# Hedgehog attention with a gated MLP on one core: the third token tile taken from the transposed copy of x, tiles 4 and 5 split one tile sooner, and the key-value products in five runs

## The chip, the core and the metric

The kernel runs on one core of one Trainium2 chip. The metric is the device time of one execution in microseconds (us), lower is better. Runs of this kernel differ by a few tenths of a microsecond.

## What is computed

x holds 2048 tokens of 640 numbers. It is normalised token by token (`xn = layernorm(x)`), and two branches use the result:

```python
q, k, v = split(xn @ wqkv)                 # 32 heads of 20 numbers
phi_q = [softmax(q @ w_phi), softmax(-q @ w_phi)]      # 40 numbers a head; phi_k likewise
kv = phi_k^T v ;  z = sum of phi_k         # sums over all 2048 tokens
s  = (phi_q kv / (phi_q z + 1e-6)) @ wo
g  = silu(gelu(xn @ w1 + b1) @ w2 + b2)
out = x + s * g
```

All is float32. The products are made of rounded parts: each operand is split into a high part (rounded) and a low part (what the rounding left), and a product takes the three passes high-high, high-low and low-high.

## The kernel before, in words

**Tiles and stages.** The tokens stand in 16 tiles of 128 (t = 0 to 15), two tiles make a pair (q = t // 2). The first stage, some 237 us long, makes for every tile the key features (`project(t, wk_s)`, `feat1`, `feat2`, `key_fin`), the values (`value(t)`, later `value_pair`), the query features, and the sums kv. Then come twelve units of the MLP (TensorE lines L987 and L1016) and the closing products with wo. This case touches the first stage alone.

**How a tile of x becomes an operand.** TensorE needs the normalised x with its 640 features on the partitions, split in high and low. There are two ways to it:

- *By transposing* (tiles 0, 1 and 2 before the change): the tile `xt` is loaded token by token, VectorE (DVE) makes mean and variance (`norm_a`, lines L220 to L222; the power -1/2 is GpSimd's, POOL, L223), ScalarE (ACT) or VectorE normalises it, TensorE transposes it with five products with the identity (`transpose_x`, L383), and `plain` copies the high part out (ACT, L272) and subtracts for the low part (DVE, L274).
- *From the transposed copy of x* (tile 3 alone, then by pairs): `one_load` loads the columns of the tile, `xr`, from the transposed copy of x in DRAM. Mean and factor stand one token to a partition, but are needed along the free dimension, the same on every partition. So `one_stats` writes them to DRAM (`st_dram`, L361), and reads them back into all 128 partitions (`bc`, L363); between the two SyncE's queue (SP) waits until the writing has landed. Then POOL subtracts the mean (`one_sub`, L370), DVE multiplies (`one_plain`, L374), and `plain` splits. A pair of tiles goes the same way: `load_xr` (L252, L253), `pair_stats` (L220 to L225, store L322, read-back L324), `pair_sub` (POOL, L331, two instructions), `pair_mul` (DVE, L336), `pair_plain`.

**What a tile's products need.** `project` and `value` take a tile's split x as the stationary operand: 30 products of 128x320 each (L397). Their result stands in one of three PSUM buffers (`bankA`), and the buffer is needed again three uses later: a key tile's is free when `feat1` has read it (DVE: maximum, difference, minimum, L409 to L415), a value tile's when ACT has copied it out (L454). `feat1` ends with a subtraction on POOL (L416), `feat2` is the exponential on ACT (L425), `key_fin` the sums and the reciprocal on DVE (L433, L465) and the scaling on POOL (L438).

**The products for kv.** `kv_acc` (L477) adds a tile's part of phi_k^T v: 64 small products of 32x40, each on 32 of TensorE's 128 columns. `kv_pair` makes two tiles in a row, 128 products, and stands at eight places of the order, one for each pair.

**Order.** The start, through tile 5 and further, is written out by hand for all engines: each engine takes its instructions in the order of the program, and one that waits holds back all that is behind it. SP issues nearly all loads and stores of this stage, in one queue, also in that order. `folds` (L156) are the weights of which `fold_pair` (TensorE L164, DVE L187 and L188) makes the query weights; their PSUM buffers are of the same three.

Of the kernel before, what the change touches and what calls it, by code (L numbers as in the profile page):

```python
# [16 lines left out]
NT = S // P  # L17
# [29 lines left out]
def hedgehog_gated_mlp_kernel(ctx: ExitStack, tc: tile.TileContext, x, xt_in, wqk, bd, wv, wo, w1, b1, w2, b2, out_t):  # L47
    nc = tc.nc
# [181 lines left out]
    def norm_a(t):  # L230
        sm = small.tile([P, 16], F32, tag="st", name="st")
        nrm[t] = sm, stats(t, sm, None, sm[:, 14:15])
# [136 lines left out]
        bc, xr = pld[t, "one"], xrs[t, "one"]  # L369
        nc.gpsimd.tensor_tensor(xr, xr, bc[:, None, :, 0].to_broadcast([P, KC, P]), op=OP.subtract)  # L370

    def one_plain(t):
        bc, xr = pld.pop((t, "one")), xrs.pop((t, "one"))
        nc.vector.tensor_tensor(xr, xr, bc[:, None, :, 1].to_broadcast([P, KC, P]), op=OP.mult)  # L374
        plain(t // 2, t % 2, xr)

    def transpose_x(t):
        q, o = divmod(t, 2)
# [101 lines left out]

    vs, es, phis, xns, wk_s, wq_s = {}, {}, {}, {}, [], [None] * 4

    def kv_pair(t):
        for u in (t, t + 1):
            kv_acc(u, phis.pop(u), vs.pop(u))

    def load_w1(g):
# [45 lines left out]
    def x_in(t, eng=None):  # L533
        xts[t] = load_x(t, eng)
# [13 lines left out]
    wv_raw = [load_raw(wv[c * P:(c + 1) * P, :]) for c in range(KC)]  # L548
    for t in (3, 4, 5):
        x_in(t)  # L550
    x_in(6)
    x_in(7)
    nc.sync.dma_start(b1t[:], b1)
    nc.sync.dma_start(b2t[:], b2)
    wv_s = []

    def split_v(c):
# [11 lines left out]
    norm_a(1)  # L569
    fold_w(wkT, range(4, KC), "wk", wk_s)  # L570
    norm_act(1)
    norm_a(2)
    st3 = one_stats(3)
    next(st3)
    split_v(0)
    one_load(3)
    kvp[0] = bankB("kv")
    pk = project(0, wk_s, lambda: transpose_x(1), 4)
    split_v(1)
    next(st3)  # L580
    load_xr(2)
    norm_act(2)
    split_v(2)
    es[0] = feat1(pk)
    split_v(3)
    pk = project(1, wk_s, lambda: transpose_x(2))
    split_v(4)
    feat2(es[0])
    es[1] = feat1(pk)
    one_sub(3)  # L590
    pair_stats(4)
    vs[0] = value(0)
    pair_stats(5)
    wqT = load_fold(0, (nc.sync,) * KC)
    x_in(8)
    x_in(9)
# [3 lines left out]
    one_plain(3)  # L600
    phis[0] = key_fin(es.pop(0))
    vs[1] = value(1)
    phis[1] = key_fin(es.pop(1))
    vf = [v_forms(0), v_forms(1)]
    for t in range(2, 6):
        pk = project(t, wk_s)
        if t % 2:
            kv_pair(t - 3)
        es[t] = feat1(pk)
        if t == 4:  # L610
            next(vf[0])
        if t == 2:
            pair_sub(2)
            pair_stats(6)
            pair_stats(7)
            pair_mul(2)
        if t == 3:
            pair_plain(2)
        if t > 3:
            pair_stats(t + 4)  # L620
        if t in (3, 4, 5):
            spill(t - 3)
        if t == 5:
            x_in(10)
        if t == 4:
            pair_sub(3)
            pair_mul(3)
        vs[t] = value(t)
        if t >= 4:
            fold_pair(t - 4)  # L630
        if t == 5:
            next(vf[0])
        feat2(es[t])
        if t == 4:
            pair_plain(3)
        phis[t] = key_fin(es.pop(t))
# [122 lines left out]
    for t in range(6, 10):  # L759
        q = t - 3  # L760
        pk = project(t, wk_s)
        if t == 8:
            kv_pair(6)
            spill(3)
        if t == 9:
            vb = value_forms(sv_raw, [nc.vector, nc.vector, nc.gpsimd, nc.gpsimd])
            w_dump(0)
            w_dump(1)
        if t == 6:
            next(vf[1])  # L770
        es[t] = feat1(pk)
        if t > 6:
            feat2(es[t])
            if t < 9:
                pair_mul(q)
                pair_plain(q)
                t_sums(q)
        else:
            pair_sub(4)
            fold_w(wqT, range(4, KC), "wq", wq_s)  # L780
            feat2(es[t])
        if t < 8:
# [24 lines left out]
        if t == 9:  # L807
            for _ in range(4):
                next(vb)
        if t == 7:  # L810
            pair_sub(5)
        if t < 9:
            store_e(queries_done.pop(0), ef)
        if t == 6:
            kv_pair(4)
        for u in XIN.get(t, ()):
            x_in(u)
    qf, later, last_sums = None, [], []
# [18 lines left out]
    for p in range(5, 8):  # L837
        t = 2 * p
# [4 lines left out]
            next(qf)  # L843
        es[t] = feat1(pk)
        pk = project(t + 1, wk_s)
        if p > 6:
            kv_pair(t - 2)
        es[t + 1] = feat1(pk, later)
        if p == 5:
            value_pair(4, {1: first_store, 2: lambda: next(vb, None), 4: x_mid, 5: lambda: plain_hi(6), 6: x_low})  # L850
# [9 lines left out]
        def between(p=p):  # L860
            if p == 5:
                load_xr(7)
                pair_stats(14)
                pair_stats(15)
            if p < 7:
                kv_pair(2 * p - 2)

        def rest(t=t, p=p):
            later.pop(0)()
# [53 lines left out]
    for q in range(4, 8):  # L923
# [4 lines left out]
            hooks[4] = last_key  # L928
        ea, eb = token_pair(q, wq_b, wq_f, hooks, later)
        if q == 5:  # L930
            kv_pair(NT - 2)
            kvr = kv_rest()
    later.pop(0)()
    e_14, e_last = ea, eb
# [685 lines left out]
```

## Time and profile before

| what | value |
|---|---|
| median of the runs | 639.14 us (639.01 to 639.66) |
| the profiled execution | 637.78 us, its span 636.1 us |
| TensorE busy | 631.3 us, 99% of the span |
| VectorE, GpSimd, ScalarE busy | 511.1, 432.5 and 259.7 us |
| DMA, mean over the span | 215 GB/s |

In the profile PE is TensorE's products and PEld its weight loads; DVE is VectorE, ACT ScalarE, POOL GpSimd, SP SyncE, and a q behind a name is the engine's issuing queue. A row of the timeline has the start, the busy time, the engine, the line, the operation, what it writes and reads, and in brackets for how long the engine stood idle ahead of it and what ended that. The chain is the work that ended last, followed back from the end. All times are from the start of the span.

### The profile page before, as it was taken

How to read it: one execution, taken by the hardware profiler on the slowest of the kernel's cores; microseconds unless marked ns; L12 is line 12 of the kernel's file. 1: busy time of each engine (PE TensorE's matmuls, PEld its weight loads, DVE VectorE, ACT ScalarE, POOL GpSimd, SP SyncE). 2: the span in 40 equal slices, each digit the busy share in tenths (PEclk: the TensorE clock that was granted, in tenths of full speed). 3: DMA queues.
4: the chain of work that ended last, by engine and by line, in shares of the span. 5: the costliest groups of instructions: out<-in, count | busy, mean ns of one | idle time of the engine just before them, and what ended most of it. 6: DMA issues, size and time to landing. Idle time of an engine off the chain costs nothing.

```text
span 636.1 us, 11441 instructions
## 1 busy us (share of the span) xinstructions
PE 631.3 (99%) x4324; PEld 550.3 (87%) x4324; DVE 511.1 (80%) x790; ACT 259.7 (41%) x390; POOL 432.5 (68%) x376
## 2 busy tenths in 40 slices
PE   9999999999999999999999999999999999999997
PEld 9999999999999998888888888888888888667676
DVE  5887976789887877878979869758798899887586
ACT  3522422334344347243442534842322335455540
POOL 1877466888978857687878876381735678866363
PEclk9999999999999999999999999999999999999999
DMA  9577287393421488359899699697498598969934
GB/s 347 121 227 230 75 286 223 100 344 134 90 76 42 131 304 284 111 106 349 212 287 315 162 385 350 135 319 258 138 245 168 172 176 271 306 181 310 377 110 152
DMA packets 167168, 136.90 MB, mean 215 GB/s; under 512 B 89864, under 2 KB 130824, under 8 KB 166728
## 3 DMA queue, kind: packets, MB, share of 16 engines
q1 hardware_dynamic: 164376, 124.56, 65.9%
q10 hardware_dynamic: 2736, 11.60, 4.7%
q8 instruction: 34, 0.56, 0.4%
q14 instruction: 22, 0.18, 0.1%
HBM read 87.76 MB, written 48.38 MB: 214 GB/s over the span
## 4 chain that ended last, share of the span: by engine, by line
PE 98%; DMA 1%; DVE 0%; SPq 0%; issue 0%
PE pB L1016 26%; PE pB L987 23%; PE pA L397 22%; PE pB L1218 10%; PE pA L710 7%; PE pB L1144 3%; PE pA L164 2%; PE qV L710 2%; PE kv L477 2%; PE qY L710 1%; DMA folds<-in_wqk_dram 1%; PE pB L1126 0%; PE pA L383 0%; DVE y L1228 0%; PE pB L942 0%; DVE xres L1229 0%
## 5 line engine op out<-in xcount | busy, mean ns | idle before, releaser
L1016 PE MATMUL pB<-hs,w2s 128*128 128x512 f32 x720 | 165.9, 389 | 0.0
L1016 PEld LDWEIGHTS pB<-hs,w2s 128*128 128x128 f32 x720 | 135.0, 188 | 28.8 <-issue 0.8
L987 PE MATMUL pB<-xp,w1s 128*128 128x512 f32 x324 | 81.4, 389 | 0.0
L987 PE MATMUL pB<-xd,w1s 128*128 128x512 f32 x324 | 79.3, 389 | 0.0
L438 POOL TENSOR_TENSOR eq<-eq,rc 128x1280 f32<-128x1280 f32 x16 | 37.9, 2371 | 60.6 <-DVE rc L1078 48.4
L987 PEld LDWEIGHTS pB<-xp,w1s 128*128 128x128 f32 x324 | 60.7, 188 | 12.8 <-ACT x L1003 0.3
L987 PEld LDWEIGHTS pB<-xd,w1s 128*128 128x128 f32 x324 | 60.8, 188 | 12.6
L1025 DVE TENSOR_TENSOR y<-pB,y 128x512 f32<-128x512 f32 x100 | 63.1, 675 | 1.8 <-PE pB L1016 1.8
L992 ACT ACTIVATE pB<-pB,b1t 128x512 f32<-128x512 f32 x48 | 31.8, 662 | 77.3 <-DVE pB L1418 29.5
L397 PE MATMUL pA<-wk,xp 128*128 128x320 f32 x384 | 59.6, 310 | 0.0
L425 ACT ACTIVATE e<-e 128x1280 f32<-128x1280 f32 x32 | 40.7, 1271 | 43.3 <-POOL e L416 42.8
L397 PEld LDWEIGHTS pA<-wk,xp 128*128 128x128 f32 x384 | 56.9, 188 | 0.1
L416 POOL TENSOR_TENSOR e<-nr,e 128x640 f32<-128x640 f32 x32 | 44.8, 1402 | 15.9 <-DVE nr L415 15.5
L438 POOL TENSOR_TENSOR e<-e,rc 128x1280 f32<-128x1280 f32 x16 | 38.4, 2407 | 21.0 <-DVE rc L465 21.0
L1065 POOL TENSOR_TENSOR ez<-eq,zrep 128x1280 f32<-128x1280 f32 x16 | 47.4, 2962 | 2.8 <-DMA eq<-e_dram 2.8
L505 POOL TENSOR_TENSOR w1s<-raw,w1s 128x640 fp32r<-128x640 f32 (+1 forms) x18 | 25.4, 1410 | 18.0 <-ACT w1s L504 17.7
L139 POOL TENSOR_TENSOR w2s<-raw,w2s 128x640 fp32r<-128x640 f32 x23 | 36.1, 1589 | 0.2 <-ACT w2s L137 0.2
L998 DVE TENSOR_TENSOR hs<-pB,hs 128x512 fp32r<-128x512 f32 x48 | 32.0, 683 | 3.8 <-ACT hs L994 3.6
L137 ACT ACTIVATE w2s<-raw 128x640 fp32r<-128x640 f32 x24 | 17.2, 735 | 41.5 <-DVE dn L433 12.1
L409 DVE TENSOR_REDUCE mx<-pA 128x32 f32<-128x640 f32 x32 | 25.9, 809 | 8.9 <-PE pA L397 8.6
L994 ACT ACTIVATE hs<-pB 128x512 fp32r<-128x512 f32 x48 | 28.8, 600 | 2.1
L397 PE MATMUL pA<-wq,xp 128*128 128x320 f32 x192 | 29.6, 309 | 0.0
(220 smaller groups left out, 1281.0 us busy)
## 6 DMA issues: line engine op xcount, KB each, us to landing
raw<-in_w_dram SPq DMA_DIRECT2D x42, 320.0 KB
e_dram<-e ACTq DMA_DIRECT2D x16, 640.0 KB
eq<-e_dram SPq DMA_DIRECT2D x16, 640.0 KB
phi_t<-eq SPq DMA_DIRECT2D x64, 160.0 KB
phT<-phi_t SPq DMA_DIRECT2D x20, 512.0 KB
xt<-in_x_dram SPq DMA_DIRECT2D x16, 320.0 KB
xres<-in_xt_dram SPq DMA_DIRECT2D x20, 256.0 KB
out_dram<-xres SPq DMA_DIRECT2D x19, 256.0 KB
```

The source lines that it names most:

```text
L139: eng.tensor_tensor(sl[:, 1, :], raw, sl[:, 0, :].bitcast(F32), op=OP.subtract)
L397: nc.tensor.matmul(ps[:, hf, :HALF], stat_x(q, o, k, a), ws[k][:, b, hf * HALF:(hf + 1) * HALF], start=n == 0, stop=n == 3 * KC - 1)
L416: rest = lambda: nc.gpsimd.tensor_tensor(e5[:, :, :, 1, :], nr[:, :, :, None].to_broadcast([P, 2, 16, DH]), e5[:, :, :, 0, :], op=OP.subtract)
L425: nc.scalar.activation(ef, ef, AF.Exp)
L438: nc.gpsimd.tensor_tensor(e3, e3, rc[:, :, None].to_broadcast([P, 64, DH]), op=OP.mult)
L710: nc.tensor.matmul(bank[ch], q_x(blk, a, q), p_weight(base, f, w, k)[:, b], start=ch not in seen and n == 0, stop=n == len(mms) - 1, skip_ ...
L987: nc.tensor.matmul(bank[ch][:], tl[:, a, off + wo_:off + wo_ + P], mov(blk, b), start=new and n == 0, stop=n == len(mms) - 1, skip_group_c ...
L998: nc.vector.tensor_tensor(hs[:, 1], ps, hs[:, 0].bitcast(F32), op=OP.subtract)
L1016: nc.tensor.matmul(ps[:], ws[i][:, b, d * P:(d + 1) * P], hs[o][i][:, a, :], start=i == n == 0, stop=(i, n) == (GF - 1, 2), skip_group_che ...
L1025: nc.vector.tensor_tensor(y, ps[:], y, op=OP.add)
L1065: nc.gpsimd.tensor_tensor(zv, ef, zf, op=OP.mult)
L1218: nc.tensor.matmul(ps[:, mv], w, o[:, mv], start=first and n == 0, stop=last and n == len(steps) - 1, skip_group_check=True)
```

## The change

Three things are changed.

1. Tile 2 is no longer transposed on TensorE. It goes by `one_load(2)`, `one_stats(2)`, `one_sub(2)`, a multiplication on DVE (`one_mul`, cut out of `one_plain`) and `plain`, whose low part stands behind `pair_stats(5)` on DVE. The loads of b1 and b2 move from ahead of tile 3's statistics to behind their read-back, and tile 3's `one_load` from ahead of the statistics' stores to between those of tile 2 and of tile 3.
2. The subtraction and the split of the pair 2 (tiles 4 and 5) come sooner: `pair_sub(2)` ahead of `key_fin` of tile 1, `pair_plain(2)` in the loop's turn for tile 2, not 3.
3. The key-value products are made in five runs: tiles 0 to 3, 4 to 7, 8 and 9, 10 to 13, 14 and 15. `kv_pair(t)` becomes `kv_tiles(*ts)`.

```diff
     def one_mul(t):
         bc, xr = pld.pop((t, "one")), xrs.pop((t, "one"))
         nc.vector.tensor_tensor(xr, xr, bc[:, None, :, 1].to_broadcast([P, KC, P]), op=OP.mult)
-        plain(t // 2, t % 2, xr)
+        return xr
+
+    def one_plain(t):
+        plain(t // 2, t % 2, one_mul(t))
...
-    def kv_pair(t):
-        for u in (t, t + 1):
+    def kv_tiles(*ts):
+        for u in ts:
             kv_acc(u, phis.pop(u), vs.pop(u))
...
     for t in (3, 4, 5):
         x_in(t)
+    one_load(2)
     x_in(6)
     x_in(7)
-    nc.sync.dma_start(b1t[:], b1)
-    nc.sync.dma_start(b2t[:], b2)
...
     norm_act(1)
-    norm_a(2)
+    for _ in one_stats(2):
+        pass
     st3 = one_stats(3)
     next(st3)
+    one_load(3)
     split_v(0)
-    one_load(3)
     kvp[0] = bankB("kv")
     pk = project(0, wk_s, lambda: transpose_x(1), 4)
     split_v(1)
     next(st3)
+    nc.sync.dma_start(b1t[:], b1)
+    nc.sync.dma_start(b2t[:], b2)
     load_xr(2)
-    norm_act(2)
     split_v(2)
     es[0] = feat1(pk)
     split_v(3)
-    pk = project(1, wk_s, lambda: transpose_x(2))
+    pk = project(1, wk_s)
     split_v(4)
+    one_sub(2)
     feat2(es[0])
     es[1] = feat1(pk)
     one_sub(3)
     pair_stats(4)
+    x2 = one_mul(2)
     vs[0] = value(0)
+    plain(1, 0, x2, lo=False)
     pair_stats(5)
+    plain(1, 0, x2, hi=False)
...
     vs[1] = value(1)
+    pair_sub(2)
     phis[1] = key_fin(es.pop(1))
...
         pk = project(t, wk_s)
-        if t % 2:
-            kv_pair(t - 3)
+        if t == 5:
+            kv_tiles(0, 1, 2, 3)
...
         if t == 2:
-            pair_sub(2)
             pair_stats(6)
             pair_stats(7)
             pair_mul(2)
-        if t == 3:
             pair_plain(2)
...
         if t == 8:
-            kv_pair(6)
+            kv_tiles(4, 5, 6, 7)
             spill(3)
```

The other three places where a `kv_pair` stood are treated in the same way.

In SP's queue this is the part from the first loads of x to the read-back for the pair 2 before the change (`xt` is x by tokens, `xr` columns of the transposed copy, `st_dram` the store of the statistics, `bc` their read-back; L347 is `one_load(3)`, L361 and L363 are tile 3's store and read-back, L322 and L324 the pair's):

```order
L132 DMA xt<-in_x_dram 128x640 x5
L553 DMA b1t<-in_b_dram 128x12
L554 DMA b2t<-in_b_dram 128x5
L347 DMA xr<-in_xt_dram 128x5x128
L361 DMA st_dram<-st 128x2
L363 DMA bc<-st_dram 128x256
L252 DMA xr<-in_xt_dram 128x5x128
L253 DMA xr<-in_xt_dram 128x5x128
L322 DMA st_dram<-pst 128x2x2
L324 DMA bc<-st_dram 128x512
```

And this is the same part after it; the first L347 and the first L361 and L363 are tile 2's, the second ones tile 3's:

```order
L132 DMA xt<-in_x_dram 128x640 x3
L347 DMA xr<-in_xt_dram 128x5x128
L132 DMA xt<-in_x_dram 128x640 x2
L361 DMA st_dram<-st 128x2
L363 DMA bc<-st_dram 128x256
L347 DMA xr<-in_xt_dram 128x5x128
L361 DMA st_dram<-st 128x2
L363 DMA bc<-st_dram 128x256
L584 DMA b1t<-in_b_dram 128x12
L585 DMA b2t<-in_b_dram 128x5
L252 DMA xr<-in_xt_dram 128x5x128
L253 DMA xr<-in_xt_dram 128x5x128
```

A second store and read-back now stand ahead of tile 3's, and tile 3's load stands between the two.

On POOL this is the part from tile 3's subtraction to the first subtraction of `feat1` for tile 2, before the change (L223 is the power for tiles 4 and 5, L438 the scaling of `key_fin`, here for tiles 0 and 1, L331 the pair 2):

```order
L416 TENSOR_TENSOR e<-nr,e 128x32x20
L370 TENSOR_TENSOR xr<-xr,bc 128x5x128
L223 TENSOR_TENSOR pst<-pst,mhalf 128x1
L447 MEMSET v 128x32
L448 MEMSET v 128x32
L223 TENSOR_TENSOR pst<-pst,mhalf 128x1
L438 TENSOR_TENSOR e<-e,rc 128x1280
L447 MEMSET v 128x32
L448 MEMSET v 128x32
L438 TENSOR_TENSOR e<-e,rc 128x1280
L416 TENSOR_TENSOR e<-nr,e 128x32x20
L331 TENSOR_TENSOR xr<-xr,bc 128x5x128 x2
```

And after it, behind tile 2's subtraction (L370 is still tile 3; L419 and L441 are the lines that were L416 and L438):

```order
L419 TENSOR_TENSOR e<-nr,e 128x32x20
L370 TENSOR_TENSOR xr<-xr,bc 128x5x128
L223 TENSOR_TENSOR pst<-pst,mhalf 128x1
L450 MEMSET v 128x32
L451 MEMSET v 128x32
L223 TENSOR_TENSOR pst<-pst,mhalf 128x1
L441 TENSOR_TENSOR e<-e,rc 128x1280
L450 MEMSET v 128x32
L451 MEMSET v 128x32
L331 TENSOR_TENSOR xr<-xr,bc 128x5x128 x2
L441 TENSOR_TENSOR e<-e,rc 128x1280
L419 TENSOR_TENSOR e<-nr,e 128x32x20
```

The pair's subtraction now stands ahead of the scaling of tile 1 and of tile 2's subtraction in `feat1`, and those two are behind it.

More of the change, by code (lines that the diff above doesn't have):

```diff
@@ L370, in one_sub, with one_mul @@
         nc.gpsimd.tensor_tensor(xr, xr, bc[:, None, :, 0].to_broadcast([P, KC, P]), op=OP.subtract)
-    def one_plain(t):
+    def one_mul(t):
         bc, xr = pld.pop((t, "one")), xrs.pop((t, "one"))
         nc.vector.tensor_tensor(xr, xr, bc[:, None, :, 1].to_broadcast([P, KC, P]), op=OP.mult)
-        plain(t // 2, t % 2, xr)
+        return xr
+    def one_plain(t):
+        plain(t // 2, t % 2, one_mul(t))
     def transpose_x(t):
@@ L813, in hedgehog_gated_mlp_kernel @@
             store_e(queries_done.pop(0), ef)
-        if t == 6:
-            kv_pair(4)
         for u in XIN.get(t, ()):
@@ L845, in hedgehog_gated_mlp_kernel @@
         pk = project(t + 1, wk_s)
-        if p > 6:
-            kv_pair(t - 2)
+        if p == 7:
+            kv_tiles(10, 11, 12, 13)
         es[t + 1] = feat1(pk, later)
@@ L864, in between @@
                 pair_stats(15)
-            if p < 7:
-                kv_pair(2 * p - 2)
+            if p == 5:
+                kv_tiles(8, 9)
         def rest(t=t, p=p):
@@ L930, in hedgehog_gated_mlp_kernel @@
         if q == 5:
-            kv_pair(NT - 2)
+            kv_tiles(14, 15)
             kvr = kv_rest()
```

## The prediction

> **What bounds the kernel now.** I read the chain of work that ended last, then TensorE's own waits over the whole span.
>
> ```profile
> PE 98%; DMA 1%; DVE 0%; SPq 0%; issue 0%
> ```
> ```profile
> PE pA L541 <- PEq L1610: 0.8, 1, 0.8
> PE pA L164 <- DMA folds<-in_wqk_dram: 0.2, 1, 0.2
> ```
>
> TensorE is the chain, and past the first 8 us it waits for nothing. So whatever time TensorE's own work loses comes off the end, and every wait that the change gives it is added. The other engines have slack, but an unknown amount, so the question is whether the new path of tile 2 still delivers in time. The profiled execution took 637.78 us, 1.36 below the median of the three timed runs (639.14); I sum against it and carry the difference to the median.
>
> **What TensorE saves.** The chain in order of time has the transposes of tile 2, and a run of kv products with its neighbours:
>
> ```profile
> 20.65 0.55 PE pA L383 x5
> 21.20 23.76 PE pA L397 x162
> ...
> 62.32 4.40 PE pA L397 x30
> 66.72 1.32 PE kv L477 x124
> 68.04 4.59 PE pA L397 x30
> ```
>
> The transposes' 0.55 us go. The kv products stay, but three runs fewer are begun and ended. The 30 products behind a run take 4.59 us, against 4.40 elsewhere: a run costs 1.32 + 0.19 = 1.51. Inside a run, counted in two windows that start together:
>
> ```profile
> 45.10:45.30 0.20, 0.20 (x44) 0.20 (x33) 1.00 0.95 356
> 45.10:45.70 0.60, 0.60 (x89) 0.60 (x78) 1.00 1.02 370
> ```
>
> 45 more in 0.4 us is 8.9 ns each, 1.14 us for 128. So a run's two ends cost 1.51 - 1.14 = 0.37 us (at least the 0.19 that shows behind it), and three runs fewer give 1.1 (0.6 to 1.1). Together TensorE saves 1.65 us. If all else stays hidden, that is the result.
>
> **What the other engines lose: tile 2's trip through DRAM.** Here are SP's issues for tile 3 (20.77, 23.94), for the pair 2 (31.69, 34.94) and for the pair 3 (46.36, 51.64). Each read-back is issued when its store has landed. Below them, the bytes that moved in two windows.
>
> ```profile
> 20.77 0.34 SPq L361 DMA_DIRECT2D st_dram<-st  x1
> 23.94 0.33 SPq L363 DMA_DIRECT2D bc<-st_dram  x1
> 24.32 0.43 SPq L252 DMA_DIRECT2D xr<-in_xt_dram  x1
> ...
> 31.69 0.37 SPq L322 DMA_DIRECT2D st_dram<-pst  x1
> 34.94 0.34 SPq L324 DMA_DIRECT2D bc<-st_dram  x1
> ...
> 40.10 0.38 SPq L252 DMA_DIRECT2D xr<-in_xt_dram  x1
> ...
> 46.36 0.82 SPq L322 DMA_DIRECT2D st_dram<-pst  x1
> 51.64 0.34 SPq L324 DMA_DIRECT2D bc<-st_dram  x1
> ```
> ```profile
> 24.30:27.30 3.00, 3.00 (x22) 3.00 (x22) 2.90 (x6) 1.28 (x1) 2.41 (x2) 1.00 0.69 18
> 27.30:30.40 3.10, 3.10 (x23) 3.10 (x22) 1.50 (x8) 1.87 (x2) 1.98 (x3) 1.00 0.92 244
> ```
>
> A store's trip is 3.17 and 3.25 us, and 5.28 for the third, which was issued behind four loads of xr. And the loads issued at 24.3 moved next to nothing (18 GB/s) until 27.3, while the read-back ahead of them ran; then they ran at 244. So the queue serves in order of issue, loads and stores alike: what stands behind a read-back waits 3.4 us from that one's issue. POOL's rows give the read-backs' landing and what follows:
>
> ```profile
> 16.61 0.55 POOL L223 TENSOR_TENSOR st<-st,mhalf 128x1 f32<-128x1 f32 x1 [1.62 <-DVE st L222]
> ...
> 28.80 1.59 POOL L370 TENSOR_TENSOR xr<-xr,bc 128x640 f32<-128x640 f32 x1 [1.12 <-DMA bc<-st_dram]
> ...
> 37.28 2.37 POOL L438 TENSOR_TENSOR e<-e,rc 128x1280 f32<-128x1280 f32 x1
> 39.61 1.28 POOL L416 TENSOR_TENSOR e<-nr,e 128x640 f32<-128x640 f32 x1
> 40.84 3.15 POOL L331 TENSOR_TENSOR xr<-xr,bc 128x640 f32<-128x640 f32 x2
> ...
> 58.07 1.28 POOL L416 TENSOR_TENSOR e<-nr,e 128x640 f32<-128x640 f32 x1
> ```
>
> A read-back for a tile takes 28.80 - 23.94 = 4.86 us; for a pair 5.16 (34.94 until SP's next issue, which waited for it, at 40.10). Now the new order, step by step.
>
> - Tile 2's store can be issued at 17.2, when POOL's power is done. Two loads of 320 KB (its own xr and x_in(7)) are not yet through. Four cost the pair 3's store 2.1 us, so two cost 1.05: landed at 17.2 + 3.17 + 1.05 = 21.4 (20.4 with a free queue, 22.5 by the longest trip). Read-back 21.4 to 26.3; subtraction to 27.9. With 0.82 and 0.81 us on DVE and 0.74 on ACT (rows below, same shapes) it is split by about 30.3, or by 31.1 if DVE first finishes `pair_stats(5)`. TensorE needs it at 31.2: 72 of the 162 products (0.147 each) after 21.20, less 0.55. No wait, but no room.
> - Tile 3's store is issued 0.8 behind tile 2's read-back, at 22.2, and behind tile 3's xr. That load gets the queue at 21.4 + 3.4 = 24.8 and needs 320 KB at 244 GB/s, 1.3 us. The store follows at 26.1; of its trip the part after its turn is unknown, at most 3.2; I take 2.5: landed 28.6 (25.4 if nothing held it, 29.3 at most). Read-back to 33.5, where tile 3 had its own at 28.80.
> - The pair 2's powers stand behind tile 3's subtraction on POOL. SP's store came 2.89 us after that began (28.80 to 31.69), so now at 36.4; landed 39.6; read-back until 44.8. POOL subtracts until 47.95, where it ended at 43.99 before. That would be 4 us late, and what moved ahead makes it worse: tile 1's scaling (2.37) and tile 2's subtraction (1.28), which ran before 40.9, now come behind it.
>
> What follows is priced by these rows of DVE, ACT and PE:
>
> ```profile
> 44.02 1.49 DVE L336 TENSOR_TENSOR xr<-xr,bc 128x1280 f32<-128x1280 f32 x1 [2.43 <-POOL xr L331]
> ...
> 53.17 1.49 DVE L433 TENSOR_REDUCE rc<-e 128x64 f32<-128x1280 f32 x1 [0.59 <-ACT e L425]
> ...
> 56.14 0.82 DVE L412 TENSOR_TENSOR e<-pA,mx 128x640 f32<-128x640 f32 x1
> 57.00 0.82 DVE L415 TENSOR_REDUCE nr<-e 128x32 f32<-128x640 f32 x1
> ...
> 62.95 1.49 DVE L336 TENSOR_TENSOR xr<-xr,bc 128x1280 f32<-128x1280 f32 x1 [3.85 <-POOL xr L331]
> ...
> 66.86 0.49 DVE L188 TENSOR_TENSOR sr<-sr,pA 128x320 f32<-128x320 f32 x1
> ```
> ```profile
> 45.55 0.74 ACT L272 ACTIVATE xp<-xr 128x640 fp32r<-128x640 f32 x1 [3.09 <-DVE xr L336]
> ...
> 46.50 0.51 ACT L272 ACTIVATE xp<-xr 128x384 fp32r<-128x384 f32 x1
> ...
> 50.88 0.71 ACT L454 ACTIVATE v<-pA 128x640 f32<-128x640 f32 x1 [3.87 <-PE pA L397]
> 51.87 1.27 ACT L425 ACTIVATE e<-e 128x1280 f32<-128x1280 f32 x1 [0.28 <-POOL e L416]
> ```
> ```profile
> 50.68 4.56 PE L397 MATMUL pA<-wk,xp 128*128 128x320 f32 x30
> ...
> 67.97 2.02 PE L397 MATMUL pA<-wv,b 128*128 128x320 f32 x12
> ```
>
> - *Tile 4's projection.* `pair_mul(2)` ends at 49.45, the three high parts at 50.95 (45.51 to 47.01 before), and behind them, on ACT, stands the copy of tile 2's value, to 51.7. The projection takes that PSUM buffer. TensorE would be there at 50.68 - 0.55 - 1.51 (the kv run of tiles 0 and 1 is gone from here) = 48.6. First wait: 3.1 us.
> - *Tile 5's projection.* POOL comes to tile 2's subtraction at 50.3, ends at 51.6; exponential on ACT behind the copy, 53.0. DVE from the head sums to the end of the next tile's minimum: 53.17 to 57.82 before, 4.65, now 57.65. Tile 3's subtraction (1.28) and exponential: 60.2. From head sums to tile 4's difference, 3.79: 64.0. This frees the buffer that the projection takes; TensorE would be there at 62.32 - 2.06 + 3.1 = 63.4. Second wait: 0.6.
> - *Tile 5's value.* Tile 4's minimum ends at 64.85, then POOL's subtraction starts; pair 3's began 1.75 later (58.07, then 59.82) and DVE's multiplication 3.13 after that: 69.75. The query weights' differences that free the PSUM buffer end 4.40 after it (62.95 to 67.35): 74.15. TensorE would be there at 67.97 - 0.92 + 3.7 = 70.75. Third wait: 3.4.
>
> So value(5) starts at 74.15 instead of 67.97, 6.2 late; two more merged runs give back 0.74 later. Sum: +5.45, 643.2 against the profiled execution, **644.6** against the median.
>
> **Edits at nothing.** b1 and b2, first used after 230 us, and x_in(6), (7), used at 38.9: their later loads are covered. Phi and values held longer keep buffers: `load_xr(5)` now waits for tile 4's kv product.
>
> ```profile
> 117.68 1.39 PE L477 MATMUL kv<-e,v 128*32 128x40 f32 x128
> ```
>
> That is at 118.4 by this clock; a pair needs about 4 us, so POOL's `pair_sub(5)`, at 120.97 before, comes 1.5 late. That run is now 256 products and holds TensorE 1.14 us longer at the same place, so I price it at 0 (at most 1.5).
>
> **The rivals.**
>
> *A, the trips are covered.* The late chain costs nothing if the pair's read-back lands by 37.6 (44.8, less the 7.1 us that TensorE waits and 0.1); it breaks even at 39.3. Then the time is 639.14 - 1.65 = 637.5. For it: SP's store for tile 2 starts 3.5 us sooner than tile 3's did. Against: two trips in a row of 3.2 and 4.9, measured. The Trainium skill, "DMA: Bandwidth & Descriptors", section on the anatomy of one DMA, gives about 2.0 us and bytes at 436 GB/s for a DMA; that would be 2.3 us for tile 2's read-back and bring the pair's in time, 637.5. The rows (3.17 for 1 KB, 4.86 for 128 KB) do not agree, and they decide. Chance 0.17.
>
> *B, the store is not held.* Tile 3's store passes the read-back and the load ahead of it and lands at 25.4, 3.2 sooner. The first wait goes, value(5) starts at 70.95: +3.0 - 0.74, so 641.4. For it: I took the order of loads among themselves from a clear row, that of a store behind loads from one trip of 5.28. Chance 0.2, a quarter of it within 0.2% of 639.14.
>
> *C, the clock falls too.* The waits of 3.1 and 3.4 us are the first pauses of TensorE since the start; the granted clock is 1.00 in all windows above. If it fell to a half for as long as each wait lasted, half of 6.5 us more is lost: 647.9. No row here shows a lowered clock. The Trainium skill, "TensorE: Matmul & The Clock Gate", "Why this matters for your kernels", warns of just this for idle gaps above some 3 us; no run so far shows it. Chance 0.12.
>
> *The forecast* has what remains, 0.51.
>
> **How the numbers follow.** About 0.2%, 1.3 us, is what a measurement of this kernel can tell from no change. Faster is A, 0.16 of it beyond 1.3 us; within it a rest of A, B's quarter and a little of the forecast, 0.08; slower 0.76. The range leaves out A and B's lower end (some 0.19) and holds forecast, B and C: 640.0, since B with tile 2's store at 20.4 gives 641.4 - 1.0 and some of its buffers' slack, to 648.2, just above C; tile 2's store at 22.5 would add 1.1 to the forecast.
>
> **What would show it.** Right: DMA waits on POOL ahead of all three, tile 2's, tile 3's and the pair 2's subtraction, the last near 44.8; TensorE idle ahead of tile 4's projection (ended by ACT's copy of a value) and of tile 5's value (ended by DVE's L188 subtraction); kv runs without a pause of their own. Wrong: TensorE without a wait after 8 us, or the pair 2's read-back landing by 40, which would put the fault in the two trips; or a wait at tile 2's own projection at 31.2, which would put it in the first.

## The result, and the profile after the change

| | before | after |
|---|---|---|
| median of 6 runs, us | 639.12 (638.97 to 639.66) | 655.01 (651.26 to 657.85) |
| ratio | | 1.0247, 95% interval 1.0215 to 1.0278 |
| profiled execution, us (span) | 637.78 (636.1) | 656.25 (654.5) |
| mean granted clock of TensorE | 1.000 | 0.989 |

The change made the kernel 2.5% slower: 15.9 us by the medians, 18.4 by the two profiled spans. The forecast was 644.6, its range ended at 648.2. TensorE's waits (total, how often, longest):

```profile
PE pA L400 <- ACT v L457: 6.5, 1, 6.5
PE kv L480 <- issue: 6.2, 3, 2.4
PE pA L717 <- DVE v L731: 0.4, 1, 0.4
```

The first row is the wait at tile 4's projection, named in the forecast, twice as long. The second is new: TensorE stands idle three times *inside* the runs of key-value products, and what ends the idle time is "issue": nothing that the profile follows, no semaphore and no other engine. TensorE's timeline at these places (start, duration, line, products, idle time before):

```profile
55.59 6.54 PE L400 MATMUL pA<-wk,xp 128*128 128x320 f32 x30 [6.52 <-ACT v L457]
61.96 4.56 PE L400 MATMUL pA<-wv,xp 128*128 128x320 f32 x30
...
73.53 1.66 PE L480 MATMUL kv<-e,v 128*32 128x40 f32 x159
76.87 1.11 PE L480 MATMUL kv<-e,v 128*32 128x40 f32 x97 [1.68 <-issue]
...
126.12 2.07 PE L480 MATMUL kv<-e,v 128*32 128x40 f32 x202
130.59 0.70 PE L480 MATMUL kv<-e,v 128*32 128x40 f32 x54 [2.41 <-issue]
131.23 6.20 PE L400 MATMUL pA<-wq,xp 128*128 128x320 f32 x30
...
207.62 2.18 PE L480 MATMUL kv<-e,v 128*32 128x40 f32 x217
211.94 0.57 PE L480 MATMUL kv<-e,v 128*32 128x40 f32 x39 [2.14 <-issue]
```

Each of the three runs of 256 products breaks off once, after 159, 202 and 217 of them. The two runs of 128 have no break. And the 30 products behind the first wait take 6.54 us, those behind the second break 6.20, where 30 alike take 4.56. The windows say why. The column behind the five engines is the granted clock, as a share of the full one, on average over the window:

```profile
55.60:62.00 6.40, 6.40 (x31) 6.40 (x32) 4.84 (x7) 1.70 (x2) 4.08 (x6) 0.68 0.14 18
77.90:82.40 4.50, 4.50 (x38) 4.49 (x31) 4.47 (x7) 0.70 (x2) 0.41 (x1) 1.00 0.39 149
131.20:137.20 6.00, 6.00 (x40) 5.97 (x31) 3.83 (x5) 1.27 (x1) 5.37 (x4) 0.72 0.52 173
212.40:217.10 4.70, 4.70 (x32) 4.66 (x22) 0.00 (x0) 0.88 (x2) 1.28 (x2) 0.64 0.01 3
```

The clock is 0.68, 0.72 and 0.64 behind the first wait and the second and third break, and 1.00 behind the first break, the shortest (1.68). So each of these three pauses costs twice: its length, and 1.5 to 2 us of slower products.

How the first wait came to 6.5 us is in SP's issues (the store and read-back of tile 2, of tile 3, of the pair 2), in POOL's rows for tile 3 and the pair 2, and in DVE's multiplication and ACT's high part and value copy:

```profile
17.46 0.39 SPq L361 DMA_DIRECT2D st_dram<-st  x1
21.38 0.33 SPq L363 DMA_DIRECT2D bc<-st_dram  x1
...
22.30 0.46 SPq L361 DMA_DIRECT2D st_dram<-st  x1
28.91 0.32 SPq L363 DMA_DIRECT2D bc<-st_dram  x1
...
37.51 0.37 SPq L322 DMA_DIRECT2D st_dram<-pst  x1
42.02 0.34 SPq L324 DMA_DIRECT2D bc<-st_dram  x1
```
```profile
34.57 1.64 POOL L370 TENSOR_TENSOR xr<-xr,bc 128x640 f32<-128x640 f32 x1 [5.55 <-DMA bc<-st_dram]
...
46.63 3.17 POOL L331 TENSOR_TENSOR xr<-xr,bc 128x640 f32<-128x640 f32 x2 [3.47 <-DMA bc<-st_dram]
49.75 2.36 POOL L441 TENSOR_TENSOR e<-e,rc 128x1280 f32<-128x1280 f32 x1
```
```profile
49.83 3.63 DVE L336 TENSOR_TENSOR xr<-xr,bc 128x1280 f32<-128x1280 f32 x1 [2.42 <-POOL xr L331]
```
```profile
53.49 0.74 ACT L272 ACTIVATE xp<-xr 128x640 fp32r<-128x640 f32 x1 [14.96 <-DVE xr L336]
...
54.85 0.68 ACT L457 ACTIVATE v<-pA 128x640 f32<-128x640 f32 x1
```

The chain is the one of the forecast, link by link, and its links are longer towards the end: tile 2's trip as worked out, tile 3's read-back 1.1 late, the pair's store 4.51 us under way where 3.2 was taken, the subtraction done at 49.80 (47.95). The store's packets moved from 38.39 to 38.63, so 3.4 us lie between its last packet and its landing, where 2.1 did in the kernel before; the cause of that is open. Then DVE's multiplication of the pair, 1.49 us before, takes 3.63: POOL's scaling began 0.08 us ahead of it and ended at 52.11, and 52.11 + 1.49 = 53.60 is about where DVE ends (53.46).

Where the 18.4 us are, by the difference between the starts of the same product of TensorE in the two traces:

| place | us |
|---|---|
| wait at tile 4's projection | +6.6 |
| lower clock behind it | +2.0 |
| key-value runs: breaks 6.23, all runs together (breaks included) | +6.2 |
| lower clock behind the second and third break | +3.0 |
| tile 2's transposes | -0.5 |
| small waits (0.6 ahead of L717's products, and others) | +1.0 |

So the tile and the runs cost about half each, and over a quarter of the loss is the clock. This is the bill of one execution: the six had granted clocks of 0.989 to 0.996, and the one with 0.996 was the shortest (651.26).

### The profile page after: what moved, and what is told of

Its sections match the earlier page's. It is cut to its first block, busy times and chain, and to the rows that moved or that the text cites. A ratio compares the mean times of both kernels' runs of the same rounds, so it can differ in the third digit from the quotient of the medians.

```text
span 654.5 us, 11441 instructions
## 1 busy us (share of the span) xinstructions
PE 636.1 (97%) x4319; PEld 554.9 (85%) x4319; DVE 516.0 (79%) x791; ACT 258.7 (40%) x389; POOL 433.4 (66%) x377
## 4 chain that ended last, share of the span: by engine, by line
PE 86%; DMA 6%; DVE 3%; POOL 2%; issue 2%; ACT 0%; SPq 0%; DVEq 0%; POOLq 0%
PE pB L1021 25%; PE pB L992 22%; PE pA L400 15%; PE pB L1223 10%; PE pA L717 5%; PE pB L1149 3%; DMA bc<-st_dram 2%; PE pA L164 1%; PE kv L480 1%; PE qV L717 1%; DMA st_dram<-pst 1%; DVE xr L336 1%; DMA st_dram<-st 1%; DMA folds<-in_wqk_dram 1%; PE qY L717 1%
## 5 line engine op out<-in xcount | busy, mean ns | idle before, releaser
L441 POOL TENSOR_TENSOR eq<-eq,rc 128x1280 f32<-128x1280 f32 x16 | 37.9, 2371 | 60.6 <-DVE rc L1083 43.8
L400 PE MATMUL pA<-wk,xp 128*128 128x320 f32 x384 | 61.4, 316 | 6.5 <-ACT v L457 6.5
L400 PEld LDWEIGHTS pA<-wk,xp 128*128 128x128 f32 x384 | 58.7, 194 | 6.9 <-ACT v L457 6.8
L419 POOL TENSOR_TENSOR e<-nr,e 128x640 f32<-128x640 f32 x32 | 44.2, 1384 | 16.9 <-DVE nr L418 11.0
L441 POOL TENSOR_TENSOR e<-e,rc 128x1280 f32<-128x1280 f32 x16 | 37.8, 2367 | 21.0 <-DVE rc L468 21.0
L400 PE MATMUL pA<-wq,xp 128*128 128x320 f32 x192 | 31.1, 320 | 0.0
L400 PEld LDWEIGHTS pA<-wq,xp 128*128 128x128 f32 x192 | 30.0, 197 | 0.1
```

What stands on the lines that cost most here:

```text
L400: nc.tensor.matmul(ps[:, hf, :HALF], stat_x(q, o, k, a), ws[k][:, b, hf * HALF:(hf + 1) * HALF], start=n == 0, stop=n == 3 * KC - 1)
L419: rest = lambda: nc.gpsimd.tensor_tensor(e5[:, :, :, 1, :], nr[:, :, :, None].to_broadcast([P, 2, 16, DH]), e5[:, :, :, 0, :], op=OP.subtract)
L441: nc.gpsimd.tensor_tensor(e3, e3, rc[:, :, None].to_broadcast([P, 64, DH]), op=OP.mult)
```

## What breaks the runs: three experiments

**Theory.** The page's list of DMA queues has one that carries instructions in large pieces:

```profile
q8 instruction: 34, 0.56, 0.3%
```

34 packets, 0.56 MB: 16 KB each. TensorE's instructions in the trace, loads of weights, matmuls, semaphore instructions and drains, are 8,742, so 64 bytes and 256 to a packet. Counted from the first, the breaks stand behind instructions 1217, 2497 and 4289: five and seven times 256 apart, exactly. So TensorE's program seems to come in blocks of 256 instructions, and one block is used up before the next is there. The three packets that end the breaks start at 74.44, 128.01 and 209.72, each 1.0 to 1.1 us long, and TensorE goes on 1.3 to 1.4 us behind their end. A block of the usual products lasts 128 x 0.147 = 19 us; one of key-value products 1.4. **Rivals:** the break comes from a run's length, or has to do with tile 2's late data.

**Five runs alone.** The kernel before, with only this part of the change:

```diff
-        if t % 2:
-            kv_pair(t - 3)
+        if t == 5:
+            kv_tiles(0, 1, 2, 3)
...
-            kv_pair(6)
+            kv_tiles(4, 5, 6, 7)
...
-        if p > 6:
-            kv_pair(t - 2)
+        if p == 7:
+            kv_tiles(10, 11, 12, 13)
```

> The kernel before with only the key-value products in five runs; tile 2 is transposed on TensorE as before. Theory (TensorE's instructions come in blocks of 256, and a run of 256 products, 512 instructions at about 10 ns a product, uses one whole block up in 1.3 us, before the next is there): a pause of 1.7 to 2.4 us in each of the three merged runs, not at a fixed product, but where a block ends. Counted over the loads of weights, matmuls and semaphore instructions, that is at products 153, 196 and 210 of the 256 (give or take 2), where the changed kernel had 159, 202 and 217, because ten instructions of transposes stand ahead; with it a lower granted clock behind those over 2 us; together about 639.1 - 1.1 + 6.2 + 3.1 = 647.3 (645 to 649). No wait at tile 4's projection. Rival (the pauses in the changed kernel follow from tile 2's late data, or from the run's length alone): none here, 638.0; or at products 159, 202 and 217 again.

Measured: 647.42 (646.76 to 650.7) against 637.76 of the kernel before on that chip; ratio 1.0141 (1.0101 to 1.0181). The three merged runs in its timeline:

```profile
65.40 1.61 PE L477 MATMUL kv<-e,v 128*32 128x40 f32 x153
68.74 1.17 PE L477 MATMUL kv<-e,v 128*32 128x40 f32 x103 [1.73 <-issue]
...
118.05 2.02 PE L477 MATMUL kv<-e,v 128*32 128x40 f32 x196
122.90 0.77 PE L477 MATMUL kv<-e,v 128*32 128x40 f32 x60 [2.84 <-issue]
...
199.36 2.13 PE L477 MATMUL kv<-e,v 128*32 128x40 f32 x211
203.97 0.63 PE L477 MATMUL kv<-e,v 128*32 128x40 f32 x45 [2.48 <-issue]
```

The breaks come after 153, 196 and 211 products, as forecast (153, 196, 210), not after 159, 202 and 217; and they stand again behind instructions 1217, 2497 and 4289. Tile 2 is transposed here, so its late data have no part in it. The clock fell behind the break of 2.84 us (0.72 from 123.6 to 129.6), not behind the one of 2.48. The time grew by 9.7 us, where I gave 8.2: the breaks are 7.0 in all and the lower clock costs 1.5, half of what I had; and the 1.1 us that I took as saved by fewer runs are not there.

**Runs of three tiles.** If a block's end decides, runs of one length must differ.

```diff
-        if t % 2:
-            kv_pair(t - 3)
+        if t == 5:
+            kv_tiles(0, 1, 2)
...
-            kv_pair(4)
+            kv_tiles(3, 4, 5)
...
-        if p > 6:
-            kv_pair(t - 2)
+        if p == 7:
+            kv_tiles(10, 11, 12)
...
-            kv_pair(NT - 2)
+            kv_tiles(13, 14, 15)
```

> The kernel before with the products in six runs: of the tiles 0 to 2, 3 to 5, 6 and 7, 8 and 9, 10 to 12, 13 to 15, so four runs of 192 products alike. Theory (a run pauses where a second block of 256 instructions would begin inside it): counted from the kernel before, blocks end at product 25, 27, 82 and 110 of the four, and the next ones 128 products later: at 153 and 155 of the first two, behind the end of the other two. So a pause of 1.7 to 2.8 us in the first two, at those products, and none over 0.5 in the last two; the time is 2 to 7 us above the kernel before. Rival (a run of over 128 products pauses by its length): a pause in all four, or in none, and at like products.

Measured: 645.70 (643.41 to 646.45) against 638.82, ratio 1.0110 (1.0093 to 1.0127). The four runs of 192:

```profile
66.71 1.61 PE L477 MATMUL kv<-e,v 128*32 128x40 f32 x153
70.09 0.57 PE L477 MATMUL kv<-e,v 128*32 128x40 f32 x39 [1.77 <-issue]
...
96.79 1.63 PE L477 MATMUL kv<-e,v 128*32 128x40 f32 x155
100.42 0.56 PE L477 MATMUL kv<-e,v 128*32 128x40 f32 x37 [2.00 <-issue]
...
198.73 1.97 PE L477 MATMUL kv<-e,v 128*32 128x40 f32 x192
...
224.69 1.98 PE L477 MATMUL kv<-e,v 128*32 128x40 f32 x192
```

Four runs alike in length: breaks in the first two, at the products forecast, none in the other two. So a rule of length does not hold. The median is 6.9 us above the kernel before. The profiled execution (643.41, the fastest of four) shows 3.8 in the two breaks and a wait of 1.1 at tile 4's projection, to which TensorE comes 1.3 sooner, since the first run has been moved behind it. Its granted clock was 1.000; that of the other three, 1.6 to 3.0 us longer, was 0.994 to 0.997.

**As many instructions, each longer.** The changed kernel, each key-value product 320 columns wide; the sums kv are then other ones.

```diff
-                nc.tensor.matmul(ps[32 * e:32 * e + 32, 40 * s:40 * s + 40], v[:, 21 * h:21 * h + 32],
-                                 phi[:, 40 * h:40 * h + 40], ...
+                nc.tensor.matmul(ps[32 * e:32 * e + 32, :320], v[:, 21 * h:21 * h + 32],
+                                 phi[:, 320 * (s // 2):320 * (s // 2) + 320], ...
```

> The changed kernel with each key-value product 320 columns wide, not 40 (the key-value matrix then holds other sums, eight heads' products each): as many instructions in the same five runs, but each takes about 35 ns if four of them still run beside each other (a quarter of the 147 ns of a 128x320 product), not 10. Theory (the next block of instructions comes some 3 to 4 us after the one before it was begun): 256 instructions now last 4.5 us, so the three merged runs have no pause over 0.5 us; the time grows by the products, some 1024 x 0.025 = 26 us, less 6 to 9 of pauses and clock: about 672. Rival (a run of 256 products in this tile shape pauses whatever it lasts): three pauses of about 2 us again.

Measured: 705.01, one run. Its first merged run, in one piece:

```profile
73.30 17.43 PE L480 MATMUL kv<-e,v 128*32 128x320 f32 x256
```

No run breaks off, and TensorE's only long wait is the one at tile 4's projection (6.3). A product takes 68 ns, not 35, so the time is 33 us above what I gave. On the question asked, the theory holds: with as many instructions in a run, and each one longer, the break is gone. The Trainium skill, "Runtime: NRT & Kernel Launch", section "Instruction fetch mechanics", describes the blocks of 256 instructions, with the next one fetched while the present one runs, and calls the cost mostly hidden. The traces agree on the blocks; that they are hidden holds here for products of 147 and of 68 ns, not of 10.

## What the third tile costs: five experiments

**Tile 2 alone, eight runs.** The first run stands behind tile 4's projection, since tile 1's features come later now.

```diff
-        if t == 5:
-            kv_tiles(0, 1, 2, 3)
+        if t > 3:
+            kv_tiles(2 * t - 8, 2 * t - 7)
...
```

The other runs of four tiles are divided into runs of two in the same way.

> The changed kernel with the key-value products in eight runs of 128, as before, save that the first stands behind tile 4's projection, as tile 1's features are not ready sooner. Theory (the third tile's trip costs its own part): no pause in any run of products; TensorE waits 6.5 us ahead of tile 4's projection, until about 55.6, as in the changed kernel, then runs some 2 us of work at a lower granted clock: 639.1 - 0.55 + 6.5 + 2.0 + 0.4 = 647.4 (646 to 649). Rival (the prediction's bill, in which only the late trip counts and the clock stays): 639.1 - 0.55 + 3.1 + 0.6 + 3.4 = 645.7. Second rival (the pauses have to do with tile 2's data): pauses remain, over 651.

Measured: 646.49 (646.26 to 646.62) against 637.76, ratio 1.0116 (1.0085 to 1.0146). TensorE's two waits:

```profile
53.55 7.14 PE L400 MATMUL pA<-wk,xp 128*128 128x320 f32 x30 [4.65 <-ACT v L457]
...
75.84 1.99 PE L400 MATMUL pA<-wv,b 128*128 128x320 f32 x12 [0.86 <-ACT xp L272]
```

No run breaks off: the second rival falls. The time is 8.7 us above that of the kernel before; the theory gave 8.3, the prediction's bill 6.6. The parts are not quite mine: the pair's read-back is there 2.0 us sooner than in the profiled execution of the changed kernel (POOL begins at 44.62), so the wait is 4.65; the clock costs more behind it (0.61 from 53.6 to 60.6; 7.14 us for the 30 products); and of the third wait that the prediction named, at tile 5's value, 0.86 is there.

Within their intervals the two experiments add up: 1.41% (1.01 to 1.81) and 1.16% (0.85 to 1.46), where the whole change has 2.47 (2.15 to 2.78).

**POOL's order: the pair's subtraction last.** On the kernel of eight runs:

```diff
-    pair_sub(2)
     phis[1] = key_fin(es.pop(1))
...
         if t == 2:
+            feat2(es[t])
+            pair_sub(2)
...
-        feat2(es[t])
+        if t != 2:
+            feat2(es[t])
```

> As the run with eight runs of products, but GpSimd scales tile 1's key features and subtracts tile 2's range before it comes to the pair's subtraction, not behind it. Theory (VectorE's multiplication of the pair took 3.63 us and not 1.49 since it could not start until GpSimd's scaling beside it had ended): the multiplication takes 1.5, TensorE's wait ahead of tile 4's projection falls from 6.5 to about 4.4, time 2 to 2.5 us under that of the eight runs (about 645). Rival (3.63 is the multiplication's own, or the wait hangs on the exponential that now stands ahead on ScalarE): no change within 0.5 us, or slower.

Measured: ratio 1.0089 (1.0059 to 1.0120), against 1.0116; 644.51 where eight runs had 646.49, 2.0 less. The profiled execution of the five took 1629.03 us, for a reason that is not known; the ratio leaves it out, and nothing is read from its trace. The others took 643.81 to 645.63, all less than the shortest of eight runs (646.26). The same kernel was run once more for a profile:

> The kernel with tile 1's scaling and tile 2's range ahead of the pair's subtraction again, for its profile. Theory: VectorE's multiplication of the pair 2 takes 1.5 us, where it took 3.6 in the eight runs, and TensorE's wait ahead of tile 4's projection is some 2 us shorter than 4.65. Rival: 3.6 again, and the 2 us come from somewhere else.

646.63 in one run, on another chip, where the kernel before took 638.82: 7.8 us more, where eight runs had 8.7 more. POOL's subtraction and the two powers behind it, DVE's multiplication, TensorE's wait:

```profile
46.34 3.13 POOL L331 TENSOR_TENSOR xr<-xr,bc 128x640 f32<-128x640 f32 x2
49.42 1.99 POOL L223 TENSOR_TENSOR pst<-pst,mhalf 128x1 f32<-128x1 f32 x2
```
```profile
49.51 1.49 DVE L336 TENSOR_TENSOR xr<-xr,bc 128x1280 f32<-128x1280 f32 x1 [2.42 <-POOL xr L331]
```
```profile
53.13 6.03 PE L400 MATMUL pA<-wk,xp 128*128 128x320 f32 x30 [4.02 <-ACT v L457]
```

With only POOL's two powers of 128x1 beside it, and no scaling, DVE's multiplication takes 1.49. From the end of POOL's subtraction to TensorE's start are 3.66 us (49.47 to 53.13), in the changed kernel 5.79 (49.80 to 55.59): the 2.1 that the theory named. TensorE's wait is only 0.6 shorter than in the profile of eight runs, and not 2 as forecast, since the subtraction began later (46.34; there 44.62). Another 1.1 is the clock: the 30 products behind the wait take 6.03 us, there 7.14. The Trainium skill, "SBUF — State Buffer", section "SBUF: two separate sides", gives this rule: one of a VectorE instruction with two inputs in SBUF and a GpSimd instruction that reads SBUF blocks the other for its whole length. The rows agree: 3.63 beside the scaling, which began first, against 1.49. The profile before the change has such a row already, for a later pair beside a subtraction of POOL (124.09 to 125.36):

```profile
124.16 2.55 DVE L336 TENSOR_TENSOR xr<-xr,bc 128x1280 f32<-128x1280 f32 x1 [2.60 <-POOL xr L331]
```

**POOL's order: the powers first.** On the kernel of eight runs, the pair's powers ahead of tile 3's subtraction, which waits for a read-back:

```diff
-    one_sub(3)
     pair_stats(4)
...
     pair_stats(5)
+    one_sub(3)
```

> As the run with eight runs of products, but GpSimd does the powers of the pair's statistics before it waits for tile 3's read-back, not behind tile 3's subtraction, so that SyncE can issue the pair's store at about 32.4 and not at 37.5. Theory (the queue holds the store behind the pair's own load of x, whose packets ended at 37.5 in the changed kernel): the store lands at most 1 us sooner than 42.0, the time falls by 1 at most (646.4). Rival (the prediction's step: the store waits for GpSimd alone): it lands about 5 us sooner, TensorE waits 1.5 and the clock stays up: about 640.4.

Measured: 644.18 (643.58 to 647.13), by the medians 2.3 less than eight runs, though two of the six runs (646.60 and 647.13) are no shorter; ratio 1.0099 (1.0069 to 1.0129).

```profile
31.55 0.37 SPq L322 DMA_DIRECT2D st_dram<-pst  x1
37.10 0.34 SPq L324 DMA_DIRECT2D bc<-st_dram  x1
```
```profile
51.00 6.20 PE L400 MATMUL pA<-wk,xp 128*128 128x320 f32 x30 [2.18 <-ACT v L457]
...
73.31 1.99 PE L400 MATMUL pA<-wv,b 128*128 128x320 f32 x12 [1.82 <-ACT xp L272]
```

The store lands at 37.10, 4.9 us ahead of 42.0, as the rival said; but TensorE waits 2.2 and not 1.5, the clock does fall (0.72 from 51.0 to 57.1), and the time is 3.8 us above the rival's. GpSimd is not all that the store waits for: it is issued 4.4 us sooner than in the eight runs (31.55, there 35.91) and lands 2.8 sooner (there 39.94). It is not held behind the loads of xr, as the theory had it (its packets run beside theirs, from 32.4; the loads' until 33.7), but the last 16 of its 256 packets move at 34.6 to 34.8. At tile 4 the wait falls from 4.65 to 2.2, and now 1.8 of the prediction's third wait shows, at tile 5's value: part of what is won at the one place is lost at the next.

**Both orders, and SP's.** Besides, tile 3's load of x is issued behind tile 2's store, the pair's behind tile 3's store, the biases behind the pair's read-back:

```diff
         nc.sync.dma_start(st_dram[t // 2, t % 2], ps)
+        then()
...
-    for _ in one_stats(2):
+    for _ in one_stats(2, lambda: one_load(3)):
         pass
-    st3 = one_stats(3)
+    st3 = one_stats(3, lambda: load_xr(2))
```

> Tile 2 from the transposed copy with eight runs of products, GpSimd's order of both runs before (powers of pair 2 ahead of tile 3's subtraction; tile 1's scaling and tile 2's range ahead of the pair's), and SyncE's order so that no load stands between a store and its read-back's turn: tile 3's x behind tile 2's store, pair 2's x behind tile 3's store, the two biases behind pair 2's read-back. Theory (all of tile 2's cost is these places): pair 2's read-back lands by about 40, as in the kernel before; TensorE waits for nothing at tile 4's and 5's projections and values; the time is that of the kernel before less five transposes, 0.55: 0.1% faster, at most 0.2% either way. Rival (two trips more on one queue can't be hidden in 9 us whatever the order): a wait of 1 to 3 us stays at tile 4's projection or tile 5's value, with a lower clock behind it: 0.3 to 0.8% slower.

Measured: 646.99 (645.5 to 648.77) against 638.82, ratio 1.0127 (1.0107 to 1.0148): no better than eight runs alone (1.0116). The rival's waits and its lower clock are there, but it gave 0.3 to 0.8%.

```profile
37.17 0.33 SPq L324 DMA_DIRECT2D bc<-st_dram  x1
```
```profile
42.15 2.37 POOL L442 TENSOR_TENSOR e<-e,rc 128x1280 f32<-128x1280 f32 x1
...
45.71 3.14 POOL L331 TENSOR_TENSOR xr<-xr,bc 128x640 f32<-128x640 f32 x2
```

The pair's read-back is issued at 37.17, so with the 4.6 us that it took in the changed kernel (42.02 to 46.63) it would be there at about 41.8 (an estimate); but POOL now scales tile 1 and subtracts tile 2's range first, and comes to the pair at 45.71. The two orders work against each other: the one that brings the data sooner needs POOL free for them. TensorE waits 2.8 us at tile 4 and 2.4 at tile 5. That no order could hide the two trips, as the rival says, is not shown.

**One trip, not two.** The kernel before, with the tiles 2 and 3 changed over: tile 2 by the copy, tile 3 by transposing.

```diff
-    norm_a(2)
-    st3 = one_stats(3)
-    next(st3)
+    for _ in one_stats(2):
+        pass
+    norm_a(3)
...
-        pk = project(t, wk_s)
+        pk = project(t, wk_s, (lambda: transpose_x(3)) if t == 2 else None)
```

> The kernel before with the tiles 2 and 3 changed over: tile 2 comes from the transposed copy, with its statistics through DRAM, and tile 3 is transposed on TensorE. So tile 2's copy, store and read-back stand where the changed kernel has them, but one tile has such a trip, not two; runs of products and all else as before. Theory (what the changed kernel lost with tile 2 is the second trip in a row, which puts the pair 2's read-back behind two others): the pair 2's read-back lands by 41, TensorE waits for nothing over 0.3 us behind the start, and the time is that of the kernel before within 0.2%. Rival (tile 2 is too early for this way, or its copy crowds out the loads ahead of it): a wait at tile 2's projection or ahead of it, and 0.3% or more slower.

Measured: 640.17 (639.50 to 640.91, 10 runs) against 638.72, ratio 1.0021 (1.0012 to 1.0031). TensorE's longest wait past the start, and the pair 2's store, read-back and subtraction:

```profile
PE pA L714 <- DVE v L728: 0.8, 1, 0.8
```
```profile
32.94 0.37 SPq L322 DMA_DIRECT2D st_dram<-pst  x1
36.18 0.34 SPq L324 DMA_DIRECT2D bc<-st_dram  x1
```
```profile
41.79 3.14 POOL L331 TENSOR_TENSOR xr<-xr,bc 128x640 f32<-128x640 f32 x2 [0.68 <-DMA bc<-st_dram]
```

Tile 2 by this way, at the same place in the program, makes TensorE wait for nothing over 0.3 us at its own projection, at tile 4's or at tile 5's value; the read-back is there at 41.8, 1.7 later than in the kernel before (40.10), and still in time. So what costs is the second trip in a row, not tile 2's. Three figures of the theory are missed by a little: 0.2%, the read-back by 41, and "for nothing over 0.3 us". In this profile TensorE is 0.9 us behind the kernel before at 35 us, and loses 1.7 more at the values from 150 to 160 us (the row of 0.8).

## Why the prediction was wrong, point by point

- **Direction and first place: right.** Slower, by tile 2's trip ahead of tile 3's, with the wait at tile 4's projection ended by ACT's copy of tile 2's value. Tile 2's trip came to 0.1 us as worked out (landed 21.38, forecast 21.4; POOL at 26.21, forecast 26.3). That tile 2's own projection would just not wait held too. Rival A, all covered, and rival B, tile 3's store landing at 25.4, both fell. The figure of the Trainium skill in rival A ("DMA: Bandwidth & Descriptors") is given there for DMAs that GpSimd issues; those of this case are SyncE's, so here the rows alone count.
- **Tile 3's store: 28.91 where 28.6 was worked out, in part by luck.** It was to wait for tile 2's read-back and then for tile 3's load, since the queue was taken to serve loads and stores in order. Its packets (25.77 to 26.79) start as the read-back's end (25.78), but they run beside the load's (24.83 to 26.74). So it started 0.3 us sooner than forecast and then took 3.1 where 2.5 was taken. The pair's store with the powers first ran beside two loads as well.
- **The step that failed: "kv runs without a pause of their own", three runs fewer save 1.1 us.** They cost 6.2, with 3.0 of clock behind them. The five-runs experiment has that part alone (1.41%); the runs of three show that the place where a block of 256 instructions ends decides. I had read a run's ends from 45 products in a window, 8.9 ns each; the whole run of 153 takes 10.5 each, so there was next to nothing to save either: all runs together, less their breaks, are 0.05 us shorter than before. No rival held this, so the range left it out.
- **The first wait: right in mechanism, 6.5 where 3.1 was worked out.** Of the 3.4 missing, 2.1 are DVE's multiplication, which I moved with its old 1.49 beside a POOL instruction that I had myself placed there (shown by POOL's other order), though the profile before had it at 2.55 beside one; 1.85 are the trips, above all the pair's store (4.51, where I took 3.2); less 0.5, as TensorE came later than forecast.
- **The second and third waits (0.6 and 3.4): not there** in the changed kernel, as TensorE came to both places late enough by the first wait and the clock. With the first wait cut, 0.9 and 1.8 of the third show.
- **Rival C, the clock: right, given 0.12.** The sum itself had the clock at nothing, and it cost 5.0. I priced the rival at half of the wait; behind the first wait it cost 2.0 of 6.5. That it would also fall behind shorter pauses was not in it.
- **Tile 2's transposes:** 0.47 saved, 0.55 forecast.

The sum: 5.45 forecast, 18.4 found. To the forecast come the breaks (6.2), the clock (5.0), the longer first wait (3.4), the ends of runs not saved (1.1) and small waits (1.0); off it go the waits 2 and 3 (4.0). That gives 18.2.

Left open: what sets a break's length. In all eight the packet that ends it starts 0.6 to 1.5 us behind the first instruction of the block then running, takes 0.9 to 1.5, and TensorE goes on 1.2 to 1.5 behind its end; why one starts later than another is not known. Open too is what held the last packets of the pair's store in the run with the powers first (a block of TensorE's instructions moves just then, from 33.66 to 34.61, which was seen, not tested). No version here beats the kernel before; the most that tile 2 has to give is the 0.5 us of its transposes, and the prediction took 1.3 us as what a measurement can tell.

## What to carry to other kernels

Before many short instructions are put in one run of TensorE, count them: where a whole block of 256 had 1.4 us of work, TensorE stood still each time, however little it waited for data. The shortest of all other blocks in these traces lasted 2.9 us, and none of them broke off. A duration that is moved to another place is good there only if the neighbours on the other engines are the same. And a pause of TensorE, where it bounds the kernel, is to be priced with the slower clock that may follow.

## What the runs showed that was not expected

- **TensorE's instructions come in blocks of 256** (packets of 16 KB): from the first instruction of a block to the first of the next there are 3.1 to 4.2 us where it breaks off (1.4 us of 128 products and a break of 1.68 to 2.84). All eight breaks of three kernels stand a multiple of 256 instructions apart. That only one block is held ahead fits these breaks, but was not tested.
- **Short pauses can cost the clock, and the place of a pause decides.** Behind pauses of TensorE the granted clock falls in these traces from 1.00 to 0.50 for 3.41 us, or for twice that, and all its changes in one execution lie whole multiples of 3.41 us apart. Divide an execution into such stretches: in the eight profiles with pauses of over 1 us the clock fell at the end of every stretch in which TensorE had stood idle for 2.0 us or more, and of none with 1.73 or less; it stayed low for a second one where 1.3 us or more of that were idle too. So it fell behind pauses of 2.14, 2.18, 2.41, 2.43 and 2.84 us, of which 2.0 to 2.4 lie in one stretch, and not behind those of 2.48 and 2.76, which a border cuts in halves (1.24 and 1.24; 1.34 and 1.42). The first border lies elsewhere in each execution (3.9 to 6.7 us from its start), so with a pause of this length it is luck. This is read from the traces, and no run was made to test it. Products of 147 ns then take 267; it cost 1.5 to 2.6 us each time. The Trainium skill, "TensorE: Matmul & The Clock Gate", "Why this matters for your kernels", sets the limit for idle gaps at about 3 us; here 2.0 within one stretch were enough.
- **A VectorE product of two SBUF tensors and a GpSimd instruction held each other up.** DVE's multiplication of a pair took 3.63 us behind the start of POOL's scaling and 2.55 behind that of a subtraction, and 1.49 where POOL had only powers of 128x1; there it was POOL that took longer, 1.99 for its two powers, where two took 1.23 in the changed kernel.
